# Output projection of a cached-attention kernel with the weights held still: three products split once, four split twice, sums kept transposed

## Chip, core and metric

The kernel runs on one core of a Trainium2 chip. The metric is device time in microseconds (us) for one execution. Engines are named as in the profile: PE (TensorE matmul), PEld (its weight load), DVE (VectorE), ACT (ScalarE), POOL (GpSimd), SP (SyncE, which issues nearly all DMAs). Every engine works through its own instructions in order and waits on semaphores.

## What is computed

```python
xn = layernorm(x)                                   # x: 2048 x 512
q  = (xn @ wq) per head                             # 32 heads of 128
p  = softmax(q @ k_cache.T * 128 ** -0.5)           # 2048 x 2048 per head
s  = concat_heads(p @ v_cache) @ wo                 # 2048 x 4096 @ 4096 x 512
g  = silu(((relu(xn @ W_gate)) * (xn @ W_up)) @ W_down)
out = x + s * g
```

The change concerns `s`: the product of the head outputs with `wo`.

## The kernel before

**Order of the work.** Attention is cut into 128 blocks, four of 512 queries for each of 32 heads (`b = 4 * head + Q`). A block has eight iterations `p`: in each, PE makes one pair of score tiles (`emit_S_tile`, two matmuls of 512 columns into a slot of the ring `ps_r`), ACT takes the exponential of a pair three iterations ahead of its use, and PE multiplies an older pair of exponentials with V (`emit_PV_tile`, eight matmuls of 129 columns into `ps_acc`). The ring has three slots of two PSUM banks. At the end of a block DVE divides by the row sums (`emit_norm_block`: a reciprocal and a multiplication into `Onorm`), and SP sends the result through a DMA transpose into `OT_store`, which holds the outputs of a group of four heads, transposed. The next block's first product with V waits for that division.

**The other work** is set into the iterations by hand. `at(b, p, ...)` puts PE work that takes a ring slot before the products with V of iteration `p` of block `b`; `side` puts work of the other engines behind it; `osteps` is the work at `p = 0`. A block in `early` makes one score pair ahead, before that work. The blocks of the first group (0 to 15) carry the gated MLP and the first query projections. From block 16 on, a group of 16 blocks carries the output projection of the heads of the group before (`emit_os`), and, up to block 114, the query projection of the group after (`emit_unit`: seven "units", each an inner Strassen product of seven matmuls, which keeps a ring slot over several iterations and accumulates in PSUM while DVE reads intermediate sums). POOL makes the sums of operands for a unit (`prep_unit`) in two sets of buffers, `TI` and `SI`, used in turn.

**Output projection before.** `emit_os(g, q, step)` makes one level of Strassen's scheme in the form of seven products. For a quarter `q` of the rows it takes 128 rows of `OT_store` (or of their sums `OX`) as weights and moves 256 columns of `Wo` (or of its sums `WX`). Four steps make products 1 and 2, 6 and 5, 7 and 3, and 4; each product is 4 matmuls, so a group has 4 x 28 = 112. DVE adds each product to one to three quarters of `s_acc`, a float32 tensor of 16 row tiles of 512 columns. DVE makes `OX` (`emit_ox`), POOL scales `Wo` by 1024 and makes `WX` (`emit_wx_scale`, `emit_wx`).

**End.** The gate `g` is spilled to the output tensor's memory and read back to `g_sb` by `reload_g` in block 115, when the query projections are over. `emit_base` multiplies a row tile of the sum by `g` and adds `x`, which comes in small loads. The last group has no Strassen product: `emit_final_tile` multiplies a row tile of 128 with `Wo` in 4 matmuls of 512 columns, multiplies by `g`, adds the base and stores the tile.

Of the kernel before, what the change touches and what calls it, by code (L numbers as in the profile page):

```python
# [5 lines left out]
BF16 = mybir.dt.bfloat16  # L6
F32 = mybir.dt.float32
# [45 lines left out]
def bass_recurrent_scan__mha_block_cached__glu_gated_reglu__prompt_kernel(  # L53
# [37 lines left out]
    OSC = 1024.0  # L91
# [25 lines left out]
    with ExitStack() as es:  # L117
# [28 lines left out]
        PT = [S_([128, 2, NQ], BF16, "PT") for _ in range(NPB)]  # L146
        xn_sb = S_([128, NT, D], BF16, "xn_sb")
# [26 lines left out]
        def sm_(shape, dt, name):  # L174
# [32 lines left out]
        s_acc = at_(0, [128, NT, D], F32, "s_acc")  # L207
        OT_store = [OT0, at_(32768, [128, G, S], BF16, "OT_store")]
        OX = at_(49152, [128, 4, G // 2, NQ], F16, "OX")
        WX = [at_(57344 + 4096 * i, [128, 4, G // 2, D // 2], F16, "WX") for i in range(2)]  # L210
        UU, VV, RR = (at_(o, [128, 4, NQ], F32, "UVR") for o in (g_at - base[0], g_at - base[0] + 8192, 92160))
        TI = [[at_(o, [128, NQ], F16, "TI") for o in os_] for os_ in (
            (104448, 105472, 106496, 107520), (65536, 66560, 100352, 101376))]
        SI = [at_(o, [128, 4, Dh], F16, "SI") for o in (102400, 108544)]
        SO = at_(88064, [128, 4, DC // 2, 2, Dh], F16, "SO")
        xr_sb = at_(99328, [128, 4, D], BF16, "xr_sb")
        fin_tmp = [WX[1][:, k].rearrange("p h d -> p (h d)").bitcast(BF16) for k in range(4)]

# [28 lines left out]
        sem_xr = [newsem(16) for _ in range(4)]  # L247
# [5 lines left out]
        sem_gr = [newsem(16) for _ in range(QB)]  # L253
# [602 lines left out]
        def emit_M(items):  # L856
            if items[0][0] is emit_unit:
                emit_unit(*items[0][2:])
# [82 lines left out]
        qp3 = {18: ((1, 0), (3, 1), (5, 2)), 19: ((0, 3), (2, 4), (4, 5)), 20: ((3, 6), (5, 7))}  # L941
# [34 lines left out]
        def scale_unit_w(g, i):  # L976
            _wait(pool, wq_tok(2 * g + i))
            w = Wq_sb[i][:].rearrange("p c i e -> p (c i e)")
            wu_tok[(g, i)] = sem_uo.sig(pool.tensor_scalar(w, w, WSC, None, op0=ALU.mult))  # L979

        def sum_unit_w(g):
            _wait(pool, wu_tok[(g, 1)])
# [10 lines left out]
        def prep_unit(n):  # L993
            g, j, _ = unit_at[n]
            T, X = TI[n % 2], SI[n % 2]
            if n >= 2:
                _wait(pool, u_done[unit_at[n - 2][:2]])
            _wait(pool, wu_tok[(g, 0 if j < 3 else 2)])
# [8 lines left out]
            k1 = op(T[0][:], b12, b11)  # L1007
            k2 = op(X[:, 0], a21, a22, ALU.add)
            op(T[2][:], b22, b12)
            op(X[:, 2], a11, a21)  # L1010
            _wait(pool, k1)
            k3 = op(T[1][:], b22, T[0][:])
            _wait(pool, k2)
            k4 = op(X[:, 1], X[:, 0], a11)
            _wait(pool, k3)
            op(T[3][:], b21, T[1][:])
            _wait(pool, k4)
            u_prep[n] = op(X[:, 3], a12, X[:, 1])

        def emit_unit(n, step):  # L1020
            g, j, _ = unit_at[n]
            T, X = TI[n % 2], SI[n % 2]
            if step in (0, 4):
                u_held[n] = ring_acquire(hold=True)
            if step == 0:
                _wait(pe, u_prep[n])
# [14 lines left out]
            dest = {1: UU, 5: RR, 2: VV, 6: UU, 7: UU, 4: UU, 3: VV}[j]  # L1041
# [15 lines left out]
            if step == 0:  # L1057
# [5 lines left out]
                else:  # L1063
                    k["b"] = dv(D[2], base[:, 2, :], B, p6, k.get("add"), k["last"])
                    k["s"] = dv(D[1], base[:, 1, :], A, p1)
            elif step == 1:
# [5 lines left out]
                else:  # L1072
                    k["b"] = dv(D[3], base[:, 3, :], B, p5)
                    k["a"] = dv(dest[:, 2:4, :], dest[:, 2:4, :],
                                ps_r[:, 2 * s:2 * s + 1, :].to_broadcast([128, 2, NQ]), k["b"])
            elif step == 2:
                _wait(pe, k["b"])
                p3 = mm(B, X[:, 3, :], outer_x(j, 1, 1), False, True)
                k["b"] = dv(out(1), D[1], B, p3, k["a"])
            elif step == 3:  # L1080
                _wait(pe, k["a"])
                p2 = mm(A, outer_w(j, 1, 0), outer_x(j, 1, 0), False, True)
                k["a"] = dv(out(0), None if base is None else base[:, 0, :], A, p2)
                ring_release(u_held.pop(n), [k["b"], k["a"]])
            elif step == 4:
                p7 = mm(B, X[:, 2, :], T[2][:], True, False)
# [9 lines left out]
        def add_unit(g, j):  # L1096
            _wait(pool, u_tok["last"])
            for i in range(4):
# [5 lines left out]
                u_tok["add"] = sem_uv.sig(pool.tensor_tensor(dst, UU[:, i, :], RR[:, i, :], ALU.add))  # L1104
# [8 lines left out]
        def reload_g():  # L1113
            _wait_all(sp, [u_tok["last"], sem_gs.cur()])
            for Q in (0, 2, 1, 3):
                sem_gr[Q].sig(sp.dma_start(g_sb[:, 4 * Q:4 * Q + 4, :], out_t[:, 4 * Q:4 * Q + 4, :]))
# [169 lines left out]
        def emit_wx_scale(g):  # L1286
            W = Wo_sb[g % 2]
            _wait(pool, wo_tok(g))
            wflat = W[:].rearrange("p h d -> p (h d)")
            k = sem_wx.sig(pool.tensor_scalar(wflat, wflat, WOSC, None, op0=ALU.mult))  # L1290
            wx_tok[(g, 0)] = k

        def emit_wx(g):
# [7 lines left out]
            k = sem_wx.sig(pool.tensor_tensor(X[:, 0], b12, b11, ALU.subtract))  # L1301
            sem_wx.sig(pool.tensor_tensor(X[:, 2], b22, b12, ALU.subtract))
            _wait(pool, k)
            k = sem_wx.sig(pool.tensor_tensor(X[:, 1], b22, X[:, 0], ALU.subtract))
            _wait(pool, k)
            wx_tok[(g, 1)] = sem_wx.sig(pool.tensor_tensor(X[:, 3], X[:, 1], b21, ALU.subtract))

        def emit_ox(g, c, i):
            O = OT_store[g % 2]
# [3 lines left out]
            a21, a22 = O[:, 0:GH, hi], O[:, GH:G, hi]  # L1313
            if i == 0:
                _wait_all(dve, t_toks(g, c))
                _wait(dve, os_tok.get("x"))
                ox_tok["k"] = sem_ox.sig(dve.tensor_tensor(OX[:, 0], a21, a22, ALU.add))
            elif i == 1:
                sem_ox.sig(dve.tensor_tensor(OX[:, 2], a11, a21, ALU.subtract))
            elif i == 2:  # L1320
                _wait(dve, ox_tok["k"])
# [543 lines left out]
```

## Time and profile before

| | |
|---|---|
| median of 3 runs | 1242.78 us (1242.57 to 1243.33) |
| the profiled execution | 1242.84 us, span of its trace 1241.5 us |
| busy share PE, ACT, DVE, POOL | 99%, 83%, 65%, 50% |
| matmuls recorded of the output projection | 784 of 256 columns |
| its additions on DVE | 264 additions and 16 copies of 128x512, mean 682 and 685 ns |
| granted TensorE clock | 1.0 |

A busy matmul in the records includes its way through the array: 512 columns show 379 ns, while one follows the other every 215 ns. The room that a stage takes on PE is therefore read from start times in the timeline or the chain, not from busy time.

### The profile page before, as it was taken

The numbers are of one execution on the slowest core, as the hardware profiler recorded it, in microseconds if no ns is written. First come the engines' busy times: TensorE is split into PE (matmuls) and PEld (weight loads), VectorE is DVE, ScalarE is ACT, GpSimd is POOL, SyncE is SP. The second block draws the span as 40 slices with busy tenths as digits, with TensorE's granted clock in tenths as the row PEclk, the third lists the DMA queues.
The fourth block names the chain that finished last, engine by engine and source line by source line (L and its number), as shares of the span: only waits on it lengthen the run. The fifth ranks groups of instructions, "written<-read, shape, count | busy, mean of one in ns | idle before, by whom it ended". The sixth has DMA issues, their size and how long they took to land.

```text
span 1241.5 us, 29139 instructions
## 1 busy us (share of the span) xinstructions
PE 1223.8 (99%) x12125; PEld 863.6 (70%) x12353; DVE 804.2 (65%) x1313; ACT 1035.3 (83%) x1108; POOL 615.1 (50%) x622
## 2 busy tenths in 40 slices
PE   9999999999999999999999999999999999999998
PEld 5466666776777777777777777777777777777775
DVE  7668778666566746675565747574666656674467
ACT  3457877667898998989988998989989999889994
POOL 3355876414735365644674366634565466430033
PEclk9999999999999999999999999999999999999999
DMA  9712431324222332333122333333222233235322
GB/s 274 159 31 36 81 78 23 52 48 104 47 48 52 65 69 53 48 69 62 40 35 51 73 62 52 48 69 69 49 52 50 47 56 48 53 68 142 60 52 78
DMA packets 254915, 82.25 MB, mean 66 GB/s; under 512 B 226368, under 2 KB 254784, under 8 KB 254784
## 3 DMA queue, kind: packets, MB, share of 16 engines
q1 hardware_dynamic: 254112, 79.98, 31.9%
q8 instruction: 98, 1.61, 0.6%
q10 hardware_dynamic: 672, 0.39, 0.1%
q14 instruction: 33, 0.27, 0.1%
HBM read 40.63 MB, written 4.19 MB: 36 GB/s over the span
## 4 chain that ended last, share of the span: by engine, by line
PE 96%; issue 2%; POOL 1%; ACT 0%; DMA 0%; DVE 0%; SPq 0%; POOLq 0%; DVEq 0%
PE ps_acc L1576 37%; PE ps_r L1467 34%; PE ps_r L1348 7%; PE ps_r L1033 5%; PE ps_r L1145 3%; PE ps_r L1206 3%; PE ps_r L901 2%; PE ps_r L720 2%; PE ps_r L716 2%; PE ps_acc L819 1%; POOL g_sb L1631 1%; ACT PT L1479 0%; DMA x_sb<-in_A_x_dram 0%; PE ps_r L1611 0%; PE ps_r L528 0%
## 5 line engine op out<-in xcount | busy, mean ns | idle before, releaser
L1479 ACT ACTIVATE PT<-ps_r 128x1024 bf16<-128x1024 f32 x1024 | 984.4, 1027 | 137.1 <-PE ps_r L1467 127.2
L1576 PEld LDWEIGHTS ps_acc<-V_sb,PT 128*128 128x128 bf16 x8192 | 550.0, 98 | 213.3 <-ACT PT L1479 2.6
L1576 PE MATMUL ps_acc<-V_sb,PT 128*128 128x129 bf16 x8192 | 638.7, 220 | 2.0
L1467 PE MATMUL ps_r<-QT_sb,KT_sb 128*128 128x512 bf16 x1836 | 564.8, 379 | 8.8
L1038 DVE TENSOR_TENSOR UVR<-UVR,ps_r 128x512 f32<-128x512 f32 (+1 forms) x228 | 168.3, 755 | 107.2 <-PE ps_r L1033 104.3
L1366 DVE TENSOR_TENSOR s_acc<-s_acc,ps_r 128x512 f32<-128x512 f32 x264 | 167.6, 682 | 11.9 <-PE ps_r L1348 11.9
L1467 PEld LDWEIGHTS ps_r<-QT_sb,KT_sb 128*128 128x128 bf16 x2048 | 160.6, 98 | 7.3 <-ACT PT L1479 0.3
L1496 DVE RECIPROCAL rz_sb<-ps_acc 128x4 f32<-128x4 f32 x127 | 23.1, 182 | 168.0 <-PE ps_acc L1576 167.1
L1005 POOL TENSOR_TENSOR TI<-xn_sb 128x512 f16<-128x512 f16 x48 | 58.2, 1212 | 126.3 <-PE ps_r L1033 126.3
L979 POOL TENSOR_SCALAR Wq_sb<-Wq_sb 128x1024 bf16<-128x1024 bf16 x12 | 33.2, 2768 | 116.3 <-DMA Wq_sb<-in_A_wq_dram 116.3
L1499 DVE TENSOR_TENSOR Onorm<-ps_acc,rz_sb 128x512 bf16<-128x512 f32 x127 | 87.8, 691 | 4.4
L1038 DVE TENSOR_TENSOR QT_sb<-UVR,ps_r 128x512 bf16<-128x512 f32 x72 | 49.5, 687 | 57.7 <-PE ps_r L1033 54.8
L1449 POOL TENSOR_TENSOR s_acc<-s_acc,xr_sb 128x512 f32<-128x512 f32 x16 | 20.6, 1308 | 98.9 <-DVE s_acc L1444 65.0
L1104 POOL TENSOR_TENSOR QT_sb<-UVR,UVR 128x512 bf16<-128x512 f32 x24 | 34.8, 1479 | 59.6 <-DVE UVR L1038 59.6
L1104 POOL TENSOR_TENSOR UVR<-UVR,UVR 128x512 f32<-128x512 f32 x24 | 29.7, 1269 | 59.5 <-DVE UVR L1038 59.5
L1005 POOL TENSOR_TENSOR TI<-xn_sb,TI 128x512 f16<-128x512 f16 x48 | 55.6, 1159 | 0.0
L1005 POOL TENSOR_TENSOR TI<-xnT 128x512 f16<-128x512 bf16 x36 | 41.6, 1154 | 23.6 <-PE ps_r L1033 22.8
L1033 PE MATMUL ps_r<-TI,SI 128*128 128x512 f16 x126 | 47.8, 380 | 0.6
L1348 PE MATMUL ps_r<-WX,OX 128*128 128x256 f16 x336 | 45.8, 273 | 0.0
L1005 POOL TENSOR_TENSOR TI<-xnT,TI 128x512 f16<-128x512 bf16 x36 | 41.7, 1158 | 0.0
L1348 PEld LDWEIGHTS ps_r<-WX,OX 128*128 128x128 f16 x336 | 32.9, 98 | 9.8
L1290 POOL TENSOR_SCALAR Wo_sb<-Wo_sb 128x2048 bf16<-128x2048 bf16 x7 | 37.5, 5363 | 0.6
(185 smaller groups left out, 1172.9 us busy)
## 6 DMA issues: line engine op xcount, KB each, us to landing
V_sb<-in_A_v_cache_dram SPq DMA_DIRECT2D x32, 512.0 KB, 4.4
Wq_sb<-in_A_wq_dram SPq DMA_DIRECT2D x16, 256.0 KB, 3.1
Wo_sb<-in_A_wo_dram SPq DMA_DIRECT2D x8, 512.0 KB, 4.6
out_dram<-g_sb SPq DMA_DIRECT2D x4, 512.0 KB, 4.7
g_sb<-out_dram SPq DMA_DIRECT2D x4, 512.0 KB, 5.6
xr_sb<-in_A_x_dram SPq DMA_DIRECT2D x16, 128.0 KB, 2.2
OT_store<-Onorm SPq DMA_TRANSPOSE x127, 2.6
Wd_sb<-in_B_W_down_dram SPq DMA_DIRECT2D x1, 1792.0 KB, 14.6
```

Of the source, the lines that this page charges most:

```text
L1005: return sem_ui.sig(pool.tensor_tensor(dst, x, y, o))
L1033: return sem_up.sig(pe.matmul(dst, lhs, rhs, start=start, stop=stop, skip_group_check=True))
L1038: dve.tensor_tensor(dst, x, ps, ALU.add))
L1104: u_tok["add"] = sem_uv.sig(pool.tensor_tensor(dst, UU[:, i, :], RR[:, i, :], ALU.add))
L1145: ins = pe.matmul(ps_r[:, bank, :], L(i), R(i), start=(i == 0), stop=(i == HC - 1))
L1290: k = sem_wx.sig(pool.tensor_scalar(wflat, wflat, WOSC, None, op0=ALU.mult))
L1348: ins = pe.matmul(ps_r[:, bank, j * DH:(j + 1) * DH], L(i), R(i), start=(i == 0 and j == 0), stop=(i == GH - 1 and j == 1))
L1366: t = dve.tensor_tensor(names[k], names[k], view(bank), op)
L1467: ins = pe.matmul(ps_r[:, 2 * s + tt, :], KT_sb[h % 2][:, t * 128:(t + 1) * 128], QT_sb[qt_slot[(h, Q)]][:], start=True, stop=True)
L1479: act.activation(PT[pb][:], ps_r[:, 2 * s:2 * s + 2, :], ACTF.Exp, scale=scale / WSC)
L1499: dve.tensor_tensor(Onorm[ob][:], o_ap, rz_sb[:].to_broadcast([128, 4, Dh]), ALU.mult))
L1576: ins = pe.matmul(o_ap, PT[pb][:, tt, j * 128:(j + 1) * 128], V_sb[vb][:, t, 0:VW], start=(t == 0 and j % 2 == 0), stop=(t == KT - 1 and j ...
```

## The change

**Which operand stands still.** The heads' outputs become the moving operand, 512 queries at a time, and 128 columns of `Wo` the weights. The result of a matmul is then transposed: output columns on the partitions, queries along the free axis. `s_acc` becomes `[128, 4, 4, 512]`, the four Strassen quarters `J` by four pieces `i` each; `gT` and `xT` hold the gate and `x` transposed, `FO` holds rows turned back by a DMA transpose.

**Seven products.** Products 1, 7 and 4 (`emit_one`) remain 8 matmuls of 512 columns each. Products 2, 6, 5 and 3 are split again: `emit_x` makes five of the seven inner products in three steps, at iterations 0, 2 and 3 of a block, in one ring slot that it keeps, and `emit_xd` makes the other two in the next block. POOL makes the eight inner sums of each (`prep_x`).

```diff
-        def emit_os(g, q, step, *banks):
...
+        one_to = {1: (0, 1), 7: (1, 2), 4: (1, 3)}
+        two_to = {2: 0, 6: 1, 3: 2, 5: 3}
+        def emit_one(g, j, r, e0, *banks):
...
+            for k, bank in enumerate(banks):
+                e = e0 + k
+                for i in range(GH):
+                    ins = pe.matmul(ps_r[:, bank, :], o_b(g, j, i, e), o_a(g, j, i, r),
+                                    start=(i == 0), stop=(i == GH - 1))
+                p = sem_op.sig(ins)
+                _wait(dve, p)
+                toks.append(acc(one_to[j], r + 2 * e, ps_r[:, bank, :]))
+        def prep_x(g, j, part):
+            Z, Y = TO, SJ
...
+                k1 = op(Z[0][:], a21, a22, ALU.add)
+                op(Z[2][:], a11, a21)
...
+        def emit_x(g, j, step):
...
+            if step == 0:
+                x_held[0] = ring_acquire(hold=True)
+                _wait(pe, x_prep[(g, j)])
...
+                p1 = mm(A, o_b(g, j, 0, 0), o_a(g, j, 0, 0), True, False)
+                p5 = mm(B, Y[:, 0, :], Z[0][:], True, False)
+                _wait(dve, p1)
+                k["A"] = acc(J, 0, A, sub)
+                _wait(dve, p5)
+                k["B"] = acc(J, 3, B, sub)
+            elif step == 1:
+                _wait(pe, k["A"])
+                p6 = mm(A, Y[:, 1, :], Z[1][:], False, False)
+                _wait(pe, k["B"])
+                p3 = mm(B, o_b(g, j, 1, 1), Z[3][:], False, True)
...
+                k["A"] = acc(J, 2, A, sub)
+                k["B"] = acc(J, 2, B, sub)
+            else:
+                _wait(pe, k["A"])
+                p7 = mm(A, Y[:, 2, :], Z[2][:], False, True)
+                t = acc(J, (1, 3), A, sub)
+                ring_tok[x_held[0]] = [k["B"], t]
+        def emit_xd(g, j, *banks):
+            pe.matmul(ps_r[:, banks[0], :], o_b(g, j, 1, 0), o_a(g, j, 1, 0), start=True, stop=True)
+            p = sem_op.sig(pe.matmul(ps_r[:, banks[1], :], SJ[:, 3, :], o_a(g, j, 1, 1), start=True, stop=True))
+            t = acc(J, (0, 1), ps_r[:, banks[0]:banks[1] + 1, :], sub)
```

**What moves with it.** The second set of `TI` and `SI` now belongs to `prep_x` (as `TO` and `SJ`), so `prep_unit` has one set and is cut into two parts with waits on the unit before. The scalings of `Wo` and `Wq` go from POOL to DVE. The fourth sum of `OX` is made late, in place, after product 6 has been used.

```diff
-            _wait(pool, wo_tok(g))
+            _wait(dve, wo_tok(g))
-            k = sem_wx.sig(pool.tensor_scalar(wflat, wflat, WOSC, None, op0=ALU.mult))
+            wx_tok[(g, 0)] = sem_wxs.sig(dve.tensor_scalar(wflat, wflat, WOSC, None, op0=ALU.mult))
-            side.setdefault((b - 2, 0), []).append((prep_unit, n))
+            side.setdefault((b - 2, 6), []).append((prep_unit, n, 0))
+            side.setdefault((b - 1, 7), []).append((prep_unit, n, 1))
+                full, part, xs = {0: (1, 0), 2: (1, 1), 3: (7, 0), 8: (7, 1)}, (1, 9, 12, 13), {2: 4, 6: 6, 5: 10, 3: 14}
```

The last line is the table of the middle groups: product 1 at blocks 0 and 2 of the group, 7 at 3 and 8, 4 at 1, 9, 12 and 13, and `emit_x` for products 2, 6, 5 and 3 at 4, 6, 10 and 14.

**End.** `reload_g` makes eight DMA transposes instead of four plain loads, and the small loads of `x` go. The finals of the first three quarters of the rows are transposed too, and are turned back on their way out; the last four row tiles stay as they were, in `gN`, with bases that are turned by DMA (`turn_base`, `sum_base`).

```diff
-            for Q in (0, 2, 1, 3):
-                sem_gr[Q].sig(sp.dma_start(g_sb[:, 4 * Q:4 * Q + 4, :], out_t[:, 4 * Q:4 * Q + 4, :]))
+            for c in range(DC):
+                cs = slice(c * 128, (c + 1) * 128)
+                sem_gr.sig(sp.dma_start_transpose(gT[:, c, :], out2[:, cs]))
+                sem_xr.sig(sp.dma_start_transpose(xT[:, c, :], x2[:, cs]))
+            sem_gn.sig(sp.dma_start(gN[:], out_t[:, NT - 4:NT, :]))
+        def emit_final_t(Q, c, bank):
...
+            def turn():
+                _wait(sp, ftok)
+                ft_tok[Q] = sem_ft[Q].sig(sp.dma_start_transpose(FO[Q % 2][:, :, c * 128:(c + 1) * 128], gT[:, c, qs]))
+            def store():
+                eng = sp if Q < QB - 2 else act
+                _wait(eng, ft_tok[Q])
+                fo_tok[Q] = sem_out.sig(eng.dma_start(out_t[:, 4 * Q:4 * Q + 4, :], FO[Q % 2][:]))
```

**Where it shows in the order of instructions.** On PE, the start of block 58, the eleventh of its group. Before (`OX` and `WX` are the sums of the two operands, `KT_sb` marks a score pair, `V_sb` the product with V):

```order
L1467 MATMUL ps_r<-QT_sb_50,KT_sb 128x512 x2
L1348 MATMUL ps_r<-Wo_sb,OX_118 128x256 x4
L1348 MATMUL ps_r<-WX_119,OX_118 128x256 x4
L1576 MATMUL ps_acc<-V_sb,PT 128x129 x8
L1467 MATMUL ps_r<-QT_sb_50,KT_sb 128x512 x2
```

The same place after (`TI_129` to `TI_132` and `SI_134` are the inner sums of `prep_x`; the moving operand stands first):

```order
L1567 MATMUL ps_r<-QT_sb,KT_sb 128x512 x4
L1466 MATMUL ps_r<-OT_store_76,WX_120 128x512
L1466 MATMUL ps_r<-TI_129,SI_134 128x512
L1676 MATMUL ps_acc<-V_sb,PT 128x129 x16
L1567 MATMUL ps_r<-QT_sb,KT_sb 128x512 x2
L1466 MATMUL ps_r<-TI_130,SI_134 128x512
L1466 MATMUL ps_r<-TI_132,WX_120 128x512
L1676 MATMUL ps_acc<-V_sb,PT 128x129 x8
L1567 MATMUL ps_r<-QT_sb,KT_sb 128x512 x2
L1466 MATMUL ps_r<-TI_131,SI_134 128x512
```

Eight short matmuls in one place have become five long ones in three places, with score pairs and products with V between them.

On DVE, block 56, the ninth of its group, up to the division at its end. Before:

```order
L1366 TENSOR_TENSOR s_acc_116<-s_acc_116,ps_r 128x2x256 x3
L1038 TENSOR_TENSOR QT_sb<-UVR_122,ps_r 128x512
L1317 TENSOR_TENSOR OX_118<-OT_store_76 128x1024
L1319 TENSOR_TENSOR OX_118<-OT_store_76 128x1024
L1038 TENSOR_TENSOR QT_sb_49<-UVR_122,ps_r 128x512
L1322 TENSOR_TENSOR OX_118<-OX_118,OT_store_76 128x1024
L1325 TENSOR_TENSOR OX_118<-OT_store_76,OX_118 128x1024
L1496 RECIPROCAL rz_sb_75<-ps_acc 128x4
```

After:

```order
L1376 TENSOR_TENSOR s_acc_116<-s_acc_116,ps_r 128x2x512 x2
L1055 TENSOR_TENSOR QT_sb<-UVR_123,ps_r 128x512
L1347 TENSOR_TENSOR OX_119<-OX_119,OT_store_76 128x2x512
L1055 TENSOR_TENSOR QT_sb_49<-UVR_123,ps_r 128x512
L1347 TENSOR_TENSOR OX_119<-OX_119,OT_store_76 128x2x512
L1596 RECIPROCAL rz_sb_75<-ps_acc 128x4
```

The additions are fewer and twice as large, and one sum of `OX` stands directly between the unit's last addition (iteration 6) and the reciprocal.

On SP, the end of the program. Before:

```order
L1504 DMA_TRANSPOSE OT_store_117<-Onorm_78 128x4x128
L1635 DMA out_dram<-g_sb 128x2x512 x2
L1504 DMA_TRANSPOSE OT_store_117<-Onorm_79 128x4x128
L1635 DMA out_dram<-g_sb 128x2x512 x4
L1635 DMA out_dram<-g_sb 128x512 x4
```

After:

```order
L1604 DMA_TRANSPOSE OT_store_117<-Onorm_79 128x4x128
L1724 DMA out_dram<-FO_139 128x4x512
L1719 DMA_TRANSPOSE FO_140<-gT_136 128x4x128 x4
L1719 DMA_TRANSPOSE FO_139<-gT_136 128x4x128 x3
L1724 DMA out_dram<-FO_140 128x4x512
L1719 DMA_TRANSPOSE FO_139<-gT_136 128x4x128
L1774 DMA out_dram<-gN_137 128x512 x4
```

The stores of row tiles are replaced by transposes and three stores of 512 KB; the third of those stands on ACT's queue.

More of the change, by code (lines that the diff above doesn't have):

```diff
@@ L1785, in bass_recurrent_scan__mha_block_cached__glu_gated_reglu__prompt_kernel @@
                     emit_sw(pr)
-            if pq == 0 and bq == (NG - 1) * GB + 4:
-                _wait(sp, u_tok["last"])
-                for k in range(4):
-                    issue_xr(k)
             if (bq, pq) == (0, 7):
```

572 lines of the change are left out of this document (343 added, 229 removed).

## Prediction

> **What bounds the kernel now.** I read the page's busy shares first, then the chain that ended last, then the table of who waited for whom, and then the chain and the timeline of single blocks.
>
> ```profile
> PE 1223.8 (99%) x12125; PEld 863.6 (70%) x12353; DVE 804.2 (65%) x1313; ACT 1035.3 (83%) x1108; POOL 615.1 (50%) x622
> PE 96%; issue 2%; POOL 1%; ACT 0%; DMA 0%; DVE 0%; SPq 0%; POOLq 0%; DVEq 0%
> ```
>
> The chain runs through PE for 96% of the span. ACT is busy 83%, but it waits, and PE does not:
>
> ```profile
> ACT PT L1479 <- PE ps_r L1467: 127.2, 209, 3.2
> ```
>
> ACT waited 127.2 us for score pairs, in 209 waits. The pieces of the chain between 500 and 520 us give what each kind of matmul takes of PE, with a middle block from the timeline (start, length, instruction) beside them:
>
> ```profile
> 500.02 0.45 PE ps_acc L1576 x8
> 500.91 0.87 PE ps_r L1348 x8
> 508.86 0.86 PE ps_r L1467 x4
> ```
> ```profile
> 637.47 0.60 PE L1348 MATMUL ps_r<-WX,OX 128*128 128x256 f16 x4
> 637.91 0.62 PE L1576 MATMUL ps_acc<-V_sb,PT 128*128 128x129 bf16 x8
> 638.36 0.59 PE L1467 MATMUL ps_r<-QT_sb,KT_sb 128*128 128x512 bf16 x2
> ...
> 643.43 0.38 PE L1033 MATMUL ps_r<-TI,SO 128*128 128x512 f16 x1
> 643.65 0.62 PE L1576 MATMUL ps_acc<-V_sb,PT 128*128 128x129 bf16 x8
> ...
> 645.85 0.60 PE L1348 MATMUL ps_r<-WX,OT_store 128*128 128x256 f16 x4
> 646.29 0.62 PE L1576 MATMUL ps_acc<-V_sb,PT 128*128 128x129 bf16 x8
> ```
>
> One matmul of 129 columns takes 0.45 / 8 = 0.056 us, one of 256 takes 0.87 / 8 = 0.109, one of 512 takes 0.86 / 4 = 0.215. Block 58 runs from 637.91 to 646.29, 8.38 us. It holds 64 products with V (3.60), 16 score tiles (3.44), 2 matmuls of a unit and 8 of the output projection (0.43 + 0.87): 8.34. PE has no gap to speak of, so a column less on PE is time less, as long as nothing new makes PE wait.
>
> ACT is the next limit. Its exponentials in the same block:
>
> ```profile
> 638.99 8.60 ACT L1479 ACTIVATE PT<-ps_r 128x1024 bf16<-128x1024 f32 x9 [0.70 <-PE ps_r L1467]
> ```
>
> Nine in a row take 8.60 us, 0.956 each, 7.64 a block. PE without other work needs 7.04 a block, so a block with under 0.60 us of other work (three matmuls of 512) is bound by ACT, if the blocks around it are too.
>
> **The columns removed.** These rows are all the matmuls of the old output projection:
>
> ```profile
> L1348 PE MATMUL ps_r<-WX,OX 128*128 128x256 f16 x336 | 45.8, 273 | 0.0
> L1348 PE MATMUL ps_r<-Wo_sb,OT_store 128*128 128x256 bf16 x224 | 29.0, 273 | 0.0
> L1348 PE MATMUL ps_r<-Wo_sb,OX 128*128 128x256 bf16 x112 | 16.8, 273 | 0.0
> L1348 PE MATMUL ps_r<-WX,OT_store 128*128 128x256 f16 x112 | 16.6, 273 | 0.0
> ```
>
> They are 784, 112 for each of seven groups: 784 x 0.109 = 85.3 us. Now a group has 3 x 8 matmuls of 512 columns for products 1, 7 and 4, and 4 x 7 for the split ones: 52, in seven groups 364, 364 x 0.215 = 78.3 us. That is -7.0 us, 1.0 a group. The last group's 64 matmuls keep their 512 columns: 0. By the table, a middle group's blocks carry 4 to 7 matmuls of 512, units included (the least are blocks 3 and 12 of a group with 4: 7.90 us, above ACT's 7.64). In the last stretch blocks 117, 119, 123 and 125 have only 2 (7.47), but each lies beside blocks of 7.9 to 8.4, so ACT can catch up: 0, and 4 x 0.17 = 0.7 if not.
>
> **DVE.** Rows for its operations, first in the timeline of block 58, then in groups:
>
> ```profile
> 637.67 1.88 DVE L1366 TENSOR_TENSOR s_acc<-s_acc,ps_r 128x512 f32<-128x512 f32 x3
> 640.98 0.69 DVE L1038 TENSOR_TENSOR UVR<-UVR,ps_r 128x512 f32<-128x512 f32 x1 [1.43 <-PE ps_r L1033]
> 645.19 0.18 DVE L1496 RECIPROCAL rz_sb<-ps_acc 128x4 f32<-128x4 f32 x1 [0.65 <-PE ps_acc L1576]
> 645.40 0.69 DVE L1499 TENSOR_TENSOR Onorm<-ps_acc,rz_sb 128x512 bf16<-128x512 f32 x1
> ```
> ```profile
> L1038 DVE TENSOR_TENSOR UVR<-UVR,ps_r 128x1024 f32<-128x1024 f32 x30 | 36.6, 1220 | 1.0
> L755 DVE TENSOR_SCALAR Wd_sb<-Wd_sb 128x3584 bf16<-128x3584 bf16 x2 | 2.8, 1417 | 0.0
> ```
>
> A group had 40 additions of 512 elements (0.64 each in a row); it now has 24 + 32 = 56 such parts, most in pairs at 1.22: 24 of them in pairs at 1.22 and of the 32 half so, 34 us against 26: about +9 us of DVE in a group of about 135 us, where DVE is 65% busy. The scalings that come from POOL cost, by L755, 1417 x 2048 / 3584 = 0.81 us once and 0.40 twice a group. Load is no limit, but places matter. I follow the x step of block 58, with t = 0 where the previous products with V end. PE: two score pairs to 0.86, two inner products to 1.29, products with V of two iterations to 2.19, a score pair to 2.62, step 1 to 3.05, products with V to 3.50, a score pair to 3.93, step 2. DVE: the division ends at 1.1, the first two additions at 1.9 and 2.5, both before step 1 needs them; the next starts at 3.05 and ends at 3.7, before 3.93; the last two end at about 5.65, and the slot comes free before PE wants it for the unit at 5.91. So 0, with margins of 0.2 to 0.3 us: a delay beyond that reaches PE.
>
> In the ninth block of each of the five middle groups the margin is gone. The unit's last addition ends at about 7.85 of 8.34 us, and then comes one sum of `OX`, directly ahead of the reciprocal. Such sums cost before:
>
> ```profile
> L1317 DVE TENSOR_TENSOR OX<-OT_store x14: 682/684/1635, 277.4 to 1157.0; 128x1024 f16<-128x1024 bf16 x14
> L1325 DVE TENSOR_TENSOR OX<-OT_store,OX x14: 692/802/1649, 282.1 to 1159.0; 128x1024 f16<-128x1024 bf16 x14
> ```
>
> (least, median, most in ns). At 0.69 the division ends at about 9.5 and PE, which arrives with its next product with V at 8.34 + 1.29 = 9.63, does not wait. At 1.65 it ends at about 10.5 and PE waits 0.9. Between least and most lie 0.95 us, less than one sum on POOL of 1.15 (row below), so I read the most as a wait for a POOL operation under way. In the ninth block a unit's second part starts on POOL at about 7.2, so I let the sum of `OX` begin at 7.2 + 1.15 = 8.35 and last 0.69; the division then ends at 10.0, a wait of 0.4: 5 x 0.4 = +2.0 us (0 to +4.4). The Trainium skill, "SBUF — State Buffer", section "Who interferes with whom", states that a VectorE instruction with two SBUF inputs contends with a GpSimd instruction that reads SBUF, and that whichever comes second is fully blocked; the spread of the two rows above agrees, 0.95 us.
>
> **POOL.**
>
> ```profile
> L1005 POOL TENSOR_TENSOR TI<-xnT 128x512 f16<-128x512 bf16 x36 | 41.6, 1154 | 23.6 <-PE ps_r L1033 22.8
> L1005 POOL TENSOR_TENSOR SI<-SO 128x128 f16<-128x128 f16 x48 | 23.3, 484 | 0.0
> L979 POOL TENSOR_SCALAR Wq_sb<-Wq_sb 128x1024 bf16<-128x1024 bf16 x12 | 33.2, 2768 | 116.3 <-DMA Wq_sb<-in_A_wq_dram 116.3
> L1290 POOL TENSOR_SCALAR Wo_sb<-Wo_sb 128x2048 bf16<-128x2048 bf16 x7 | 37.5, 5363 | 0.6
> ```
>
> Each `prep_x` adds 4 x 1.15 + 4 x 0.45 = 6.4 us, 28 of them 179 us; the two scalings take 37.5 and 33.2 away, which leaves +108. A middle group holds about 90 us of POOL work in 135. The single set of buffers gives a unit's first part (3.5 us) the time from iteration 5 of the block before its predecessor's last to iteration 1 of its own, over 10 us, and its second part (2.65) about 11. The nearest point is block 10 of a group, where `emit_wx` (4.6 us) stands ahead of a first part: start about 0.7 us before block 10, end about 7.4 into it, need at 8.6 + 1.7 = 10.3. Margin 2.9 us: 0. A wait of 0.69 us for a sum of DVE would have to meet five of the nine operations in between to use it up, so I give it nothing above.
>
> **End and DMA.**
>
> ```profile
> KT_sb<-in_A_k_cache_dram SPq DMA_TRANSPOSE x32, 4.0
> OT_store<-Onorm SPq DMA_TRANSPOSE x127, 2.6
> out_dram<-g_sb SPq DMA_DIRECT2D x4, 512.0 KB, 4.7
> out_dram<-g_sb SPq DMA_DIRECT2D x6, 256.0 KB, 2.1
> ```
> ```profile
> 1127.39 1.82 SPq L343 DMA_TRANSPOSE KT_sb<-in_A_k_cache_dram x1
> 1129.31 2.18 SPq L1116 DMA_DIRECT2D g_sb<-out_dram x4
> ```
>
> The eight transposes of the reload have the size of a transpose of K: 8 x 1.82 + 4.0 = 18.6 us. DVE's first base stands in iteration 4 of block 118, three blocks less one iteration after the reload, at 7.9 to 8.2 us a block about 23 us. Covered: 0. The last DMA transposes of `Onorm` and the next V queue behind it and have four blocks.
>
> At the very end:
>
> ```profile
> 1233.70 2.26 POOL L1631 TENSOR_TENSOR g_sb<-s_acc,WX 128x512 bf16<-128x512 f32 x2 [0.33 <-DVE WX L1624]
> 1238.20 0.69 DVE L1629 TENSOR_TENSOR g_sb<-ps_r,s_acc 128x512 bf16<-128x512 f32 x1
> ```
>
> The sum of the last transposed piece ends at 1233.70 + 2.26 = 1235.96 on before's scale. It then needs a transpose (2.6) and a store of 512 KB (2.1 by the 256 KB row, 4.7 by four at once; I take 3.5, between): 1242.1, where the trace ended at 1241.5 with the last row tile. The 512 KB store becomes the last event: about +1.0 us, rounded up for its issue (0 to +2.3).
>
> **Sum.** -7.0 + 2.0 + 1.0 = -4.0 on the profiled execution's 1242.84, which is the median of 1242.78 but for 0.06: 1238.8 us.
>
> **Rivals.** *Slower: the kept slot sets ACT's pace.* `emit_x` keeps one of three ring slots from the start of a block to about 5.65 us. With two slots a score pair waits for the exponential two pairs back, so PE could fall from its 0.88 us an iteration to ACT's 0.956: 0.076 over five iterations, 0.38 for each of 28 x steps, 10.6 us. -7.0 + 10.6 + 1.0 = +4.6: 1247.4. For it: ACT ran nine exponentials without a break in block 58. Against it: a unit keeps a slot just as long, seven times a group, and PE shows no gap. It decides once an x step costs PE over 0.21 us (6.0 / 28). Chance 0.18.
>
> *No change: DVE and POOL collide.* With 28 more preparations POOL is oftener at work beside a sum of `OX`. At the worst row each time the ninth blocks cost 4.4, and with the tail at its upper end the sum is -7.0 + 4.4 + 2.3 = -0.3: 1242.5. For it: the 1.65 us rows. Against it: elsewhere these sums stand well ahead of a division. Chance 0.11.
>
> *No change: late transposes.* If reading 256-byte pieces out of 1 KB rows doubles their time, 8 x 3.64 + 4.0 = 33 us against 23: DVE stalls in its order for up to 10 us, PE behind it for some 5 after its slots are full (half, an estimate), and the sum is +1.0: 1243.8. Nothing in the trace shows such a read. Chance 0.06.
>
> **Numbers.** A difference under 0.2%, 2.5 us, can hardly be told from none. The forecast has 0.65 and covers 1235.6 (no wait, no tail, and 0.2 of reading) to 1240.3. Faster: 0.65. Same: 0.11 + 0.06 = 0.17. Slower: 0.18. The range goes from 1235.6 to 1246.0, into the slower case for less than its full price; outside lie most of its 0.18 upwards and little below.
>
> **What would show it.** In the new profile, 364 matmuls of 512 columns at 0.215 us apart, no other change of rate; blocks of a middle group together 1.0 us shorter than before, less 0.4 at the start of the group's tenth block, where PE would wait for the division; `OX` sums at 0.7 to 1.65 us there; DVE about 75 us (seven times 9 + 1.6) and POOL about 108 us busier; the last event a store from ACT's queue. I would be wrong if PE waits for score slots in x blocks, or if DVE waits for the transposed `g` around block 118, or if inner sums of POOL release PE.

## The result: slower by 0.2%

The changed kernel takes 1245.47 us (median of 14 runs, 1244.66 to 1245.78) against 1242.70 before (14 runs): ratio 1.0021, 95% interval 1.0012 to 1.0029. The forecast was 1238.8 and faster. The profiled execution took 1245.65 us with a span of 1244.0, where before it was 1242.84 and 1241.5.

The page after the change, busy shares and the chain that ended last:

```profile
PE 1222.6 (98%) x11719; PEld 817.2 (66%) x11933; DVE 881.2 (71%) x1314; ACT 1039.8 (84%) x1108; POOL 732.8 (59%) x839
PE 94%; issue 2%; DVE 2%; POOL 1%; ACT 1%; DMA 0%; SPq 0%; DVEq 0%; POOLq 0%
```

PE's share of the chain fell from 96% to 94%, and DVE, which had none, has 2%. DVE rose by 77 us and POOL by 118, near the forecast's +9 a group and +108. In the table of waits ScalarE's largest wait for PE is still there (119.6 us, 127.2 before), and two waits of PE on DVE are new:

```profile
ACT PT L1579 <- PE ps_r L1567: 119.6, 222, 3.2
PE ps_r L1567 <- DVE s_acc L1386: 1.1, 1, 1.1
PE ps_r L1567 <- DVE UVR L1055: 0.6, 1, 0.6
```

A cut of both timelines at the first product with V of chosen blocks says where the time went (us; "forecast" spreads the prediction's terms, 1.0 of columns saved in each group's 16 blocks):

| stretch | before | after | difference | forecast |
|---|---|---|---|---|
| blocks 0 to 15 | 201.95 | 201.95 | 0.0 | 0 |
| block 16 | 8.83 | 10.32 | +1.5 | |
| blocks 17 to 31 | 132.75 | 133.39 | +0.6 | -1.0 with block 16 |
| each middle group (five) | 136.29 | 135.94 | -0.35 | -0.6 |
| blocks 112 to 127 | 133.72 | 133.88 | +0.2 | -1.0 |
| after the last product with V (the tail) | 9.57 | 11.56 | +2.0 | +1.0 |

The differences sum to +2.5, the forecast to -4.0. So there is no single cause: every stretch that the change touches misses by one to three microseconds.

**Block 16.** The timeline, all three engines together in order of time:

```profile
277.07 1.48 POOL L1327 TENSOR_TENSOR WX<-Wo_sb,WX 128x512 f16<-128x512 bf16 x1
277.46 1.64 DVE L1338 TENSOR_TENSOR OX<-OT_store 128x1024 f16<-128x1024 bf16 x1
278.52 3.16 POOL L1434 TENSOR_TENSOR TI<-OT_store 128x512 f16<-128x512 bf16 x2
279.14 1.53 DVE L1341 TENSOR_TENSOR OT_store<-OT_store 128x1024 f16<-128x1024 bf16 x1
280.59 2.47 DVE L1386 COPY s_acc<-ps_r 128x512 f32<-128x512 f32 x4
282.98 1.59 DVE L1344 TENSOR_TENSOR OX<-OT_store 128x1024 f16<-128x1024 f16 x1
283.11 0.61 PE L1567 MATMUL ps_r<-QT_sb,KT_sb 128*128 128x512 bf16 x2 [1.11 <-DVE s_acc L1386]
```

DVE's sums of this size in the same block before the change:

```profile
277.45 1.64 DVE L1317 TENSOR_TENSOR OX<-OT_store 128x1024 f16<-128x1024 bf16 x1
279.01 0.68 DVE L1319 TENSOR_TENSOR OX<-OT_store 128x1024 f16<-128x1024 bf16 x1
281.40 0.68 DVE L1322 TENSOR_TENSOR OX<-OX,OT_store 128x1024 f16<-128x1024 f16 x1
```

The first sum took 1.64 before too, beside the last sum of `WX` on GpSimd. The second and third took 0.68 and now take 1.53 and 1.59, because GpSimd now has work there (run 1 tests this): `prep_x` for product 2 is written two blocks later, but what it waits for has long been met, so it runs straight on behind `emit_wx`. The copies that free the ring slot of product 1 stand behind the first two sums and end at 283.06; PE's next score pair waits for that slot (1.28 us from the end of its matmul before), and the third sum makes the division late (0.23 more at block 17).

**Ninth block of a middle group**, the place that the prediction did name:

```profile
628.32 1.16 POOL L1015 TENSOR_TENSOR TI<-xn_sb 128x512 f16<-128x512 f16 x1 [4.59 <-PE ps_r L1050]
628.95 1.07 DVE L1347 TENSOR_TENSOR OX<-OX,OT_store 128x1024 f16<-128x1024 f16 x1
629.94 0.17 DVE L1596 RECIPROCAL rz_sb<-ps_acc 128x4 f32<-128x4 f32 x1
630.15 0.69 DVE L1599 TENSOR_TENSOR Onorm<-ps_acc,rz_sb 128x512 bf16<-128x512 f32 x1
630.98 0.61 PE L1676 MATMUL ps_acc<-V_sb,PT 128*128 128x129 bf16 x8
```

PE's two matmuls before it start at 630.27 and last 0.43, so it waits 0.28 (forecast 0.4).

**Unit steps.** In blocks 6, 10 and 14 of a group the change sets steps 4 and 5 of a unit in neighbouring iterations (two or three apart before). In block 14:

```profile
678.07 0.38 PE L1050 MATMUL ps_r<-TI,SI 128*128 128x512 f16 x1
678.55 0.69 DVE L1055 TENSOR_TENSOR QT_sb<-UVR,ps_r 128x512 bf16<-128x512 f32 x1 [0.77 <-PE ps_r L1050]
678.74 0.59 PE L1567 MATMUL ps_r<-QT_sb,KT_sb 128*128 128x512 bf16 x2
679.30 0.39 PE L1050 MATMUL ps_r<-TI,SO 128*128 128x512 f16 x1
```

Two score matmuls from 678.74 end at 679.17; step 5 starts at 679.30, once DVE's addition is over: 0.13. In blocks 6 and 10 it is 0.06 each.

**The end.** SyncE's queue from the last transposed pieces on with ScalarE's last store, then the DMA share in two stretches of the profile (the number before the last on a row):

```profile
1227.32 9.37 SPq L1719 DMA_TRANSPOSE FO<-gT  x6
1236.73 0.58 SPq L1724 DMA_DIRECT2D out_dram<-FO  x1
1237.36 1.60 SPq L1719 DMA_TRANSPOSE FO<-gT  x1
1239.01 2.04 SPq L1774 DMA_DIRECT2D out_dram<-gN  x4
1240.82 0.39 ACTq L1724 DMA_DIRECT2D out_dram<-FO  x1
```
```profile
1234.00:1238.00 4.00, 3.98 (x19) 1.59 (x17) 3.33 (x6) 0.23 (x1) 2.67 (x3) 1.00 0.52 109
1238.00:1243.00 5.00, 0.00 (x0) 0.00 (x0) 1.41 (x3) 0.00 (x0) 1.86 (x2) 0.80 0.99 298
```

The 512 KB store does become the last event. But the last piece, whose sum ends on POOL at 1236.51, gets its transpose only at 1237.36, behind the transpose before it and another store, and the transpose takes 3.4 us to its landing. In the stretch from 1238 to 1243 the 16 DMA engines are 99% busy.

### The profile page after: what moved, and what is told of

It reads as the page before. It is cut to its first block, busy times and chain, and to the rows that moved or that the text cites. A ratio compares the mean times of both kernels' runs of the same rounds, so it can differ in the third digit from the quotient of the medians.

```text
span 1244.0 us, 28869 instructions
## 1 busy us (share of the span) xinstructions
PE 1222.6 (98%) x11719; PEld 817.2 (66%) x11933; DVE 881.2 (71%) x1314; ACT 1039.8 (84%) x1108; POOL 732.8 (59%) x839
## 4 chain that ended last, share of the span: by engine, by line
PE 94%; issue 2%; DVE 2%; POOL 1%; ACT 1%; DMA 0%; SPq 0%; DVEq 0%; POOLq 0%
PE ps_acc L1676 36%; PE ps_r L1567 33%; PE ps_r L1050 5%; PE ps_r L1167 3%; PE ps_r L1406 3%; PE ps_r L1228 3%; PE ps_r L1466 2%; PE ps_r L914 2%; PE ps_r L733 2%; PE ps_r L729 2%; PE ps_acc L832 1%; ACT PT L1579 1%; PE ps_r L1497 1%; PE ps_r L1498 1%; DMA x_sb<-in_A_x_dram 0%
## 5 line engine op out<-in xcount | busy, mean ns | idle before, releaser
L1579 ACT ACTIVATE PT<-ps_r 128x1024 bf16<-128x1024 f32 x1024 | 989.0, 1025 | 133.0 <-PE ps_r L1567 119.6
L1676 PE MATMUL ps_acc<-V_sb,PT 128*128 128x129 bf16 x8192 | 632.3, 220 | 1.7
L1567 PE MATMUL ps_r<-QT_sb,KT_sb 128*128 128x512 bf16 x1849 | 557.5, 379 | 11.4 <-DVE s_acc L1386 1.1
L1376 DVE TENSOR_TENSOR s_acc<-s_acc,ps_r 128x1024 f32<-128x1024 f32 x130 | 156.7, 1218 | 32.4 <-PE ps_r L1406 20.6
L1384 DVE TENSOR_TENSOR s_acc<-s_acc,ps_r 128x512 f32<-128x512 f32 x116 | 77.4, 685 | 22.1 <-PE ps_r L1466 18.2
L1434 POOL TENSOR_TENSOR TI<-OX 128x512 f16<-128x512 f16 x28 | 31.8, 1158 | 65.1 <-issue 65.1
L1322 POOL TENSOR_TENSOR WX<-Wo_sb 128x512 f16<-128x512 bf16 x7 | 8.1, 1157 | 90.3 <-DVE Wo_sb L1312 51.1
L1123 POOL TENSOR_TENSOR QT_sb<-UVR,UVR 128x512 bf16<-128x512 f32 x24 | 29.8, 1276 | 39.9 <-DVE UVR L1055 39.9
L1143 POOL TENSOR_SCALAR gB<-gB 128x512 bf16<-128x512 bf16 x14 | 20.8, 1487 | 30.3 <-DVE gB L1173 30.3
L1434 POOL TENSOR_TENSOR TI<-OT_store 128x512 f16<-128x512 bf16 (+1 forms) x28 | 32.7, 1190 | 9.2 <-issue 9.2
```

The source lines that it names most:

```text
L1123: u_tok["add"] = u_tok[("add", i)] = sem_uv.sig(pool.tensor_tensor(dst, UU[:, i, :], RR[:, i, :], ALU.add))
L1376: t = sem_opa.sig(dve.tensor_tensor(dst, dst, sb, op))
L1384: t = dve.tensor_tensor(dst, dst, sb, op)
L1434: return sem_oi.sig(pool.tensor_tensor(dst, x, y, o))
L1567: ins = pe.matmul(ps_r[:, 2 * s + tt, :], KT_sb[h % 2][:, t * 128:(t + 1) * 128], QT_sb[qt_slot[(h, Q)]][:], start=True, stop=True)
L1579: act.activation(PT[pb][:], ps_r[:, 2 * s:2 * s + 2, :], ACTF.Exp, scale=scale / WSC)
```

## The experiments

**1 and 2: the sums of `OX`.** The first holds GpSimd back, the second moves the sums on DVE.

```
 prep_x, g == 0, j == 2:            + _wait(pool, ox_tok[(0, 0)])
 prep_unit part 1, j == 6, g > 2:   + _wait(pool, ox_tok[(g - 2, "4")])
 prep_unit part 0, j == 5, g == 2:  + _wait(pool, ox_tok[(0, "4")])
```


> VectorE's order is that of the changed kernel; only GpSimd is held back at three places until the sum of OX beside which it ran has ended: prep_x(0, 2) until ox_tok[(0, 0)], the second part of the unit for block 9 of each middle group until ox_tok[(g, "4")], the first part of the unit for block 27 until ox_tok[(0, "4")]. Theory A (the sum is held up by a GpSimd operation under way): the sums take 0.68 us again; block 16 loses about 1.1 of its 1.5 us (the two sums of WX still run beside the first sum), the wait of 0.28 us ahead of block 9 goes in five groups (-1.4), the wait of 0.76 at block 26 goes; sum about -3.2 us: 1242.3. Theory B (VectorE is late because of its own longer list, and the long rows are only where it shows): the rows shorten, but the waits stay, since the list is the same, and the time is within 0.5 us of 1245.5.


```
 middle groups, fourth sums:  - ((8, 5), (8, 6))   + ((8, 2), (8, 5))
 group 0, fourth sums:        - ((9, 2), (9, 4))   + ((9, 2), (10, 4))
 group 0, first three, c = 0: - (0, 2..4)          + (1, 2..4)
                      c = 1:  - (1, 2..4)          + (1, 5), (1, 6), (2, 4)
```


> The same three places, mended on VectorE and with GpSimd as it was: the first three sums of OX of group 0 stand in block 17 and not in 16, those of the second half after them; the fourth sums of the middle groups stand at iterations 2 and 5 of block 8 and not at 5 and 6; the second one of group 0 in block 26 and not in 25. Theory A (place decides: a sum directly ahead of the reciprocal or of copies that free a ring slot): block 16 -1.3 us, -0.28 in each of five groups, -0.76 at block 26: -3.4 in all, 1242.1. Theory B (the load of VectorE decides, so that the loss comes up at the new place): less than half of this, 1244 or more.

Measured: 1242.72 (10 runs, 1242.61 to 1242.83) and 1242.17 (1242.05 to 1242.73). Both agree with theory A: block 16 falls from 10.32 to 9.26 and to 8.90, a middle group from 135.94 to 135.70 in both (one group of the first stays at 135.90). With GpSimd held back the second and third sum, in the same place of DVE's order, take 0.68 to 0.69, and no wait is left in the ninth block:

```profile
278.96 0.69 DVE L1345 TENSOR_TENSOR OT_store<-OT_store 128x1024 f16<-128x1024 bf16 x1
281.97 0.68 DVE L1348 TENSOR_TENSOR OX<-OT_store 128x1024 f16<-128x1024 f16 x1
...
626.72 0.68 DVE L1351 TENSOR_TENSOR OX<-OX,OT_store 128x1024 f16<-128x1024 f16 x1
627.38 0.18 DVE L1602 RECIPROCAL rz_sb<-ps_acc 128x4 f32<-128x4 f32 x1
```

So 1.06 of block 16's 1.5 us, and the wait in the ninth block, are the collision and not DVE's longer list. In run 1 the first sum still takes 1.64 beside `WX`, and PE still waits 0.44 for the slot that the four copies behind it free; with the sums moved out of the way in run 2, 0.09 of that is left. With both kernels PE's wait of 0.76 us at block 26 is gone too, but the next run shows that this alone proves nothing.

**3: the tail.**

```
 store of row block 1:  - sp, ahead of flush_last_transposes   + act, behind it
 store of row block 2:  - one store of 512 columns             + 384 columns behind the third transpose, 128 behind the last
```


> Only the end is changed: the 512 KB store of row block 1 goes from SyncE's queue, where it stands ahead of the last transpose, to ScalarE's behind its last copies; the store of row block 2 is cut in 384 columns, which need not wait for the last transpose, and 128 columns. Up to the last product with V nothing moves. Theory A (the tail is the chain sum, transpose, store, with 0.6 us of issue of another store in it): the last transpose starts 0.6 to 0.7 us earlier and the last store is a quarter: the tail falls from 11.6 us to 9.5 to 10.0, the time to about 1243.7. Theory B (the transposes and stores at the end share the DMA engines, and their bytes set the end): the tail falls by less than 0.5 us.

Measured 1244.25 (10 runs). The tail fell from 11.56 to 11.27 only: theory B is nearer. The last transpose still starts 0.96 us behind its sum (0.85 in the changed kernel; each issue of a transpose holds SyncE's queue 1.2 to 2.0 us), and the store of the last quarter took 3.4 us to land where the whole one had taken 3.2. The last event is no longer this store but that of the last row tile (run 10 below shows it). The larger part of what the run gained, 0.77 us, lies at block 26, where nothing was changed. Its two engines there, first in the changed kernel, then in this one:

```profile
363.01 1.16 POOL L1015 TENSOR_TENSOR TI<-xn_sb 128x512 f16<-128x512 f16 x1 [1.47 <-PE ps_r L1050]
363.03 1.69 DVE L1347 TENSOR_TENSOR OX<-OX,OT_store 128x1024 f16<-128x1024 f16 x1
364.64 1.27 DVE L1055 TENSOR_TENSOR UVR<-UVR,ps_r 128x512 f32<-128x512 f32 x2
```
```profile
362.85 1.71 POOL L1016 TENSOR_TENSOR TI<-xn_sb 128x512 f16<-128x512 f16 x1 [1.48 <-PE ps_r L1051]
362.86 0.68 DVE L1348 TENSOR_TENSOR OX<-OX,OT_store 128x1024 f16<-128x1024 f16 x1
363.46 1.27 DVE L1056 TENSOR_TENSOR UVR<-UVR,ps_r 128x512 f32<-128x512 f32 x2
```

Both operations start within 0.02 us. In one run DVE loses and takes 1.69, and PE waits 0.76 for a slot; in the other POOL loses and takes 1.71, and PE waits for nothing. Run 7, which changes nothing there either, shows the same gain (17.28 us for blocks 25 and 26, as in run 3, and 18.06 in the changed kernel). Three of the changed kernel's own 14 runs lie at 1244.7 and ten at 1245.4 to 1245.8, a step of the same size; that it is this toss is not shown, since only one of them has a profile. The two lengths agree with the Trainium skill, "SBUF — State Buffer", section "Who interferes with whom", which calls this contention an exclusive lock: 0.68 becomes 1.69 and 1.16 becomes 1.71, whichever loses. Which engine asked first can't be read from these rows, since GpSimd's recorded start is the earlier one in both.

**4, 6 and 11: the turn without the split.** All seven products in whole pieces, 56 matmuls of 512 a group, no `prep_x`; 4 in pieces of four, one a block in blocks 0 to 13; 6 in pieces of two spread within blocks; 11 in pieces of four or two at the starts of blocks.

```
 products 2, 6, 3, 5:  - emit_x in three steps, emit_xd, prep_x   + emit_whole: like emit_one, into one key of s_acc
```


> The turn without the split: all seven products with 512 moving columns and weights stationary, 56 matmuls of 512 a group (84.5 us of them in all by 0.2156 each; the kernel before had 85.3, the changed one 78.3); no prep_x, no kept ring slot for products. Transposed finals and reload as in the changed kernel. Theory A (what the split saves in columns, 6.2 us, it loses again in waits of PE, some 6 to 7 us by the gaps in the trace): -0.8 of columns, +2.0 of tail and 0 to 1 of other places on the time before: 1244 to 1245, so the split is worth nothing. Theory B (the split is worth its columns less 2 us, and the turn itself costs): 1249 to 1251.

> The turn without the split once more, its 56 matmuls of 512 a group in 28 pieces of two, laid so that each block of a middle group holds 6 matmuls of 512 (units included); in the run before, pieces of four left blocks 14 and 15 with 2 and 4, and PE waited 0.8 us for ScalarE ahead of each of them. The sums of OX of the first group stand as in the run with the sums moved. Theory A (evenly laid, only the columns count): a middle group takes 136.29 - 0.14 = 136.15, at most 136.5, the whole 1244 to 1245.5, so that the split is worth 2 to 3 us beside the 1242.2 of the run with the sums moved, and not the 6 us of its columns. Theory B (the turned products cost more than columns, in waits of their own): a middle group over 137, the whole over 1248.

> The turn without the split a third time: 56 matmuls of 512 a group, nearly all at the start of a block, where the score pair of the next iteration is issued ahead of them; four or two of them a block, no block of a middle group with less than 4 matmuls of 512 (units included). In the two runs before, light blocks (the first) and pieces in the middle of a block, each with a ring slot of its own (the second), cost 2 to 4 us a group. Theory A (only columns count once the places are good): a middle group 136.15 to 136.5, the whole 1244 to 1245.5, so that the split is worth 0.5 to 0.8 us a group against the 135.70 of the run with the sums moved. Theory B (the turned products have waits of their own): a middle group over 137.

Measured: 1261.09, 1271.08 and 1249.18 (4 runs each). The first two say nothing of the turn, since their places spoil them (4 lies outside both theories; 6 is in theory B's range, for another reason). In 4 no product stands at the start of blocks 14 and 15, and PE waits 0.82 us ahead of each. It waits there for the division on DVE, not for ScalarE as the expectation of run 6 has it:

```profile
678.97 0.69 DVE L1617 TENSOR_TENSOR Onorm<-ps_acc,rz_sb 128x512 bf16<-128x512 f32 x1
679.81 0.61 PE L1694 MATMUL ps_acc<-V_sb,PT 128*128 128x129 bf16 x8 [0.66 <-DVE Onorm L1617]
```

In 6 every piece in the middle of a block takes a ring slot of its own, ahead of the next score pair: PE waits 0.21 us for an exponential ahead of the piece, and 0.27 behind it, where the view names no releaser:

```profile
616.28 0.59 PE L1583 MATMUL ps_r<-QT_sb,KT_sb 128*128 128x512 bf16 x2
616.92 0.11 PEld L1498 LDWEIGHTS ps_r<-OX,WX 128*128 128x128 f16 x2 [0.54 <-ACT PT L1595]
618.08 0.59 PE L1583 MATMUL ps_r<-QT_sb,KT_sb 128*128 128x512 bf16 x2
```

11 is the usable one: a middle group takes 136.69, between the bounds of the two theories, with two waits in it, 0.41 for DVE's additions and 0.15 for an exponential; the whole is 3.7 us above theory A's range. So this turn alone is 6.4 us slower than the kernel before. Run 11 has the sums of `OX` moved, so what the split is worth is read against run 2: 1249.18 - 1242.17 = 7.0 us, of which its columns are 6.0 (28 matmuls of 0.2156) and the other 1.0 what this order waits more. Whether a better order of the turn alone exists stays open.

**5 and 9: the unit's steps.** 5 sets step 4 an iteration earlier; 9 keeps the iterations and runs step 5 behind the first four products with V of its iteration.

```
 5:  - second = (5, 6) if b + 1 in x_at      + second = (4, 6) if b + 1 in x_at
 9:  x blocks, iteration 6:  - score pair, step 5, 8 products with V   + score pair, 4 products, step 5, 4 products
```


> Only the place of one step of a unit is changed: in a block that begins an x step (blocks 4, 6, 10 and 14 of a group) the unit's step 4 stands at iteration 4 and not at 5, two iterations ahead of step 5. Theory A (step 5 waits because VectorE has only one iteration for the addition between them): the waits of 0.06, 0.06 and 0.13 us in blocks 6, 10 and 14 go, 0.26 in a middle group and as much in the first: -1.5 us, 1243.9, a middle group 135.68. Theory B (with the step's slot and the unit's slot both kept, the third slot alone feeds the score pairs for longer): a wait for a slot takes their place, and a group does not get shorter, or gets longer by up to 0.4 in each of three blocks.

> The unit steps keep their iterations; in blocks 6, 10 and 14 of a group (8, 10 and 14 of the first) TensorE runs step 5 of the unit behind four of the iteration's eight products with V and not ahead of all eight, 0.22 us later. Theory A (step 5 waits for VectorE's addition by 0.06 to 0.13 us, because the round from step 4 to step 5 is an iteration of 0.88 and the addition takes 0.69 and two hand-overs): the waits go, 0.25 us in a middle group (135.68) and 0.32 in the first, -1.6 in all: about 1243.9. Theory B (what follows step 5 has no room: its additions stand ahead of the block's division and free the kept slot): the wait moves to the next score pair or to the first product with V of the next block, and a group stays at 135.9 or gets longer.

Measured: 5 takes 1246.46 (7 runs; theory B), a middle group 136.22. That is with the toss at blocks 25 and 26 won (17.4 us). The wait for DVE is replaced by one of 0.18 for a ring slot, in each of three blocks, since the x step still keeps its own:

```profile
607.87 0.59 PE L1567 MATMUL ps_r<-QT_sb,KT_sb 128*128 128x512 bf16 x2
608.47 0.10 PEld L1050 LDWEIGHTS ps_r<-TI,SI 128*128 128x128 f16 x1 [0.51 <-ACT PT L1579]
```

9 takes 1243.83 (10 runs; theory A, 1243.9 expected), a middle group 135.66: the waits are gone and come up nowhere else.

**7 and 8: the finishing operations, and all mends.**

```
 7:  emit_finish:  - block 123, iterations 1 to 5   + pieces 3, 2 in block 122, iterations 5, 6; 1, 0 in block 123, iterations 1, 2
 8:  2, 5 and 7 together, and row block 1's store of 3
```


> Only the eight finishing operations (emit_finish) are moved: for two of the four pieces from block 123 to the end of block 122, the others to iterations 1 and 2 of block 123. Theory A (they stand directly ahead of block 123's division, which ends late): PE's wait of 0.29 us at block 124 goes, blocks 120 to 124 and 124 to 126 take 0.3 less, the rest stays: about -0.3 us. Theory B (block 123 has too little of PE's work and is bound by ScalarE anyway): no change, since PE waits for an exponential instead.

> All mends in one kernel: the sums of OX moved as in the second run, unit steps spaced as in the fifth, finishing operations as in the seventh, the store of row block 1 on ScalarE's queue behind its last copies and the store of row block 2 whole. If the parts add: 1242.2 - 1.5 - 0.3 - 0.3 = 1240.1, faster than the kernel before by 0.2%. If they get in each other's way (a wait mended at one place coming up at the next): 1241.5 or more.

Measured 1248.75 (4 runs) and 1247.16 (5 runs), both misses: 7 is 3.3 us worse than the changed kernel. Its edit does just what is examined here: it sets four operations with two inputs in SBUF beside a `prep_x` and directly ahead of a division (DVE, POOL, then PE):

```profile
1183.53 1.58 DVE L1515 TENSOR_TENSOR s_acc<-s_acc 128x512 f32<-128x512 f32 x1
1184.53 1.60 POOL L1434 TENSOR_TENSOR TI<-TI,OX 128x512 f16<-128x512 f16 x1
1185.15 1.53 DVE L1519 TENSOR_TENSOR s_acc<-s_acc 128x512 f32<-128x512 f32 x1
1189.00 0.17 DVE L1596 RECIPROCAL rz_sb<-ps_acc 128x4 f32<-128x4 f32 x1
1190.04 1.81 PE L1676 MATMUL ps_acc<-V_sb,PT 128*128 128x129 bf16 x16 [2.52 <-DVE Onorm L1599]
```

In block 123 of the changed kernel they had taken 0.7 to 0.8. The wait of 2.7 us on PE cost blocks 120 to 123 4.0 us (36.80 against 32.79), more than itself; the last section says why. 8 shares this edit and that of 5, so it says nothing of the sum of the good ones.

**10: the mends that had worked**: the sums moved (2), the late step 5 (9), row block 1's store on ScalarE's queue (from 3).

> The sums of OX moved, the late step 5, and the store of row block 1 on ScalarE's queue behind its last copies, in one kernel; finishing operations and unit iterations as in the changed kernel. If the parts add: 1242.2 - 1.6 - 0.4 = 1240.2, faster than the kernel before by 0.2%; a middle group 135.45. If the late step only moves its wait: 1241.8.

Measured 1239.72 (8 runs, 1239.56 to 1239.92), ratio to the kernel before 0.9974, interval 0.9964 to 0.9984: it is faster than the kernel before, and than the changed one. The parts add. A middle group takes 135.41, -0.88 against before of the -1.0 that the columns give; blocks 16 to 31 -0.4 and the tail 11.19. On its page PE has 96% of the chain again, and DVE 1%.

The tail is still 1.6 us longer than before. The last transpose lands after 2.5 us here and the 512 KB store after 3.3, but that store is no longer the last event. The store of the last row tile ends 0.4 us behind it; first in the changed kernel, then in run 10 (the last number is the time to landing, 1.8 before the change):

```profile
out_dram<-gN SPq DMA_DIRECT2D x1, 128.0 KB, 1.9
out_dram<-gN SPq DMA_DIRECT2D x1, 128.0 KB, 3.3
```

This speaks for run 3's theory B, that the transfers at the end share the DMA engines; no run separates it from the order of the queues.

## Why the prediction was wrong

It forecast a faster kernel with 0.65, and the kernel was slower. The measured time lies inside the range up to 1246.0 by luck: the range had been stretched upwards for the kept slot, which was not seen. The mechanism of the saving held; the waits that the new order makes were put at too little:

- *The columns removed, -7.0: right.* The profile holds the weight loads of 364 matmuls of 512 for the seven groups (and 363 of the matmuls), and run 10 keeps 0.88 of the 1.0 in a middle group.
- *"Load is no limit, but places matter" (DVE): right, and applied to one place only.* The collision was priced for the ninth block of the five middle groups (0.4 forecast, 0.28 measured), and the rival "DVE and POOL collide" counted the same five. It was not followed where GpSimd runs ahead of the block in which its work is written. In block 16 and at blocks 25/26 (1.5 and 0.76) sums stand ahead of copies or additions that free a ring slot. This is the step that failed most: 2.3 us put at 0. Runs 1 and 2 show it for block 16, 1.06 as the collision and 0.4 as the order of sums and copies on DVE; run 3 shows that 25/26 is a toss.
- *"The next starts at 3.05 ... So 0, with margins of 0.2 to 0.3 us": right for the x steps, not followed for the unit beside them.* Nothing in PE's order in x steps waits, but the unit's steps, pushed into neighbouring iterations, wait 0.06 to 0.13: 0.26 a middle group, 1.6 in all. Run 9 shows it.
- *Light blocks of the last stretch, "0, and 0.7 if not": it was not 0.* PE waits for ScalarE at the starts of seven blocks from 117 to 125, 0.05 to 0.15 each, 0.6 in sum, each until 0.05 or 0.06 us after an exponential has ended; 0.29 more at block 124 (finishing operations ahead of the division) and 0.30 in block 126 were not in the sum at all. Only the waits themselves are shown here: the one test of a cause, run 7, failed, and none was made of the light blocks.
- *The end, +1.0 (0 to +2.3): measured +2.0.* The mechanism was right, the chain of sum, transpose and store. Missing were SyncE's queue (0.85) and a transpose of 3.4 where 2.6 was taken, beside the other stores; the store itself took 3.2 where 3.5 was taken. Taking one store out of the queue brought 0.3 to 0.4. What part of the rest is DMA load stays open.
- *Kept slot and ScalarE's pace, +10.6: not seen.* No x step waits for an exponential at steps 1 or 2. Run 5 shows its edge: two kept slots an iteration earlier, and PE waits 0.18.
- *Reload and GpSimd's single buffers, 0: right.* PE never waits for GpSimd or a transpose of the reload.

The forecast was -4.0 and the two profiles differ by +2.5, 6.5 us more. Of these the steps above make 5.5: 2.3 of block 16 and 25/26, 1.6 of unit steps, 1.2 of the last stretch and 1.0 of the end, less 0.6 that the ninth block cost less than forecast. The rest lies mostly in waits of 0.1 us and less, which were not followed one by one.

## What to carry to other kernels

Price an added operation at the place where its engine will run it, not where it is written: an engine with slack runs ahead, and there may meet another's operands. Before accepting a saving of a few microseconds on an engine with no gaps, go through every short operation that stands directly ahead of one for which that engine waits (a division, a copy that frees a slot), and ask what else is at work beside it. A saving that comes out smaller than forecast may still be there: the waits that ate it were 0.06 to 1.5 us each at named places, and mending them at three kinds of places brought back 5.7 us (0.8 of it at the place of the toss).

## What the runs showed of the hardware

In run 7 a long wait of PE cost more than its length. Around the wait of 2.7 us (three stretches of the profile; the granted clock is the third number from the right):

```profile
1170.00:1187.00 17.00, 16.84 (x171) 11.39 (x173) 13.58 (x16) 15.56 (x18) 6.87 (x9) 1.00 0.08 16
1190.00:1194.00 4.00, 3.74 (x29) 3.15 (x31) 3.69 (x5) 1.02 (x1) 0.24 (x1) 0.57 0.50 37
1194.00:1200.00 6.00, 5.95 (x67) 4.16 (x67) 1.60 (x4) 5.90 (x7) 0.00 (x0) 1.00 0.00 0
```

The clock granted to TensorE was 0.57 in the 4 us around the end of the wait, and from the fourth on its products with V started 0.107 to 0.111 us apart and not 0.056. Run 8 has the same edit, and blocks 120 to 123 take 36.80 there too. Behind the changed kernel's wait of 1.28 us it stayed at 1.00:

```profile
283.10:287.00 3.90, 3.77 (x36) 2.36 (x38) 3.75 (x6) 2.85 (x3) 2.96 (x5) 1.00 0.10 21
```

The Trainium skill, "TensorE: Matmul & The Clock Gate", section "What's actually happening", gives half clock as the state behind at least one idle window of about 3.4 us. The half clock agrees; the length does not, since 2.7 us without a matmul were enough here.
